# A fused attention, transform and mixer kernel: the last batch's transform begun after the attention's steps, two product blocks ahead of it, and the first normalization spread over the steps

## The chip, the cores and the metric

The kernel runs on one core of a Trainium2 chip, with its five engines: TensorE (PE, matmuls; PEld is its weight load), VectorE (DVE), ScalarE (ACT), GpSimd (POOL) and SyncE (SP, which issues the transfers). Each engine runs its own queue in order, and engines wait for each other by semaphores. The metric is the time of one execution on the device in microseconds, median of three runs; smaller is better.

## The reference

Batch 4, 8 heads, 576 tokens, head size 64, model width 512. Three parts follow each other, the output of one being the input of the next:

```python
# attention in a window of 64 tokens
scores = where(mask, scale * q @ k.T, -1e9)
x = softmax(scores) @ v                      # heads side by side: (4, 576, 512)
# first mixer
mixed = real(fft(fft(x, axis=1), axis=2))
u = x + mixed
un = (u - mean(u)) / sqrt(var(u) + 1e-6)
x = u + relu(un @ w_ch1) @ w_ch2             # 512 -> 2048 -> 512
# second mixer
u = x + (relu(x.T @ w_tok1) @ w_tok2).T      # over the tokens, 576 -> 256 -> 576
out = u + relu(u @ w_ch1) @ w_ch2            # 512 -> 1536 -> 512
```

The weights come as 64-bit floats.

## The kernel before

**Attention, steps.** The work is cut into 36 units (4 batches, 9 units each: a tile of 128 tokens and half the heads). `front_body` runs 39 steps k, software-pipelined: in step k ScalarE does the exponentials of unit k (`a_ex`), TensorE transposes the result of unit k-1 into `pt` (`a_pt`) and multiplies that of unit k-2 by the values into `o` (`a_pv`), VectorE divides (`a_nx`), and TensorE makes the scores `s` of unit k+1, whose row maxima `mx` VectorE takes and ScalarE scales to `nb`. Everything in the front is put into each engine's queue in the order of the code (`manual_schedule`); the rest of the program is ordered by a scheduler.

**Transform.** As soon as a batch's units are done, VectorE folds its rows (`fold`, `fold_m`: tiles pmt, eo, then xh and xs, the latter for the last 64 rows, each split into a high and a low part by a ScalarE cast and a VectorE subtraction, L128 and L131). `fft(b)` is a generator of 16 pieces: the first-stage products `zp` (L531; eight matmuls in two pieces each), `zpx`, and then `bp` and `ap`, after each of which VectorE and GpSimd add the result to x. `chunk()` hands out the next piece; each step takes two.

**Normalization and first product.** `prep` yields part by part: row statistics (L664), an inverse root in small VectorE operations (L638 to L647), then for each of three tiles the normalized rows `una` (ScalarE, L679), their transposition `tpa` (TensorE, L685) and the split into `aT`. A group is 384 tokens. `side0` holds the generator of group 0, `pre1` that of group 1. In the steps, parts are taken while a budget of VectorE time, `left`, lasts. `gphase` then runs, for group g and feature block f, a first product `zg` (L694, 12 matmuls), its relu on ScalarE (L701) and VectorE's low part `hh` (L702), and, three blocks later, the second product into `acc` (L712, 9 matmuls). Called one zg block at a time, it makes 32 such blocks for groups 0 and 1, in the middle with the groups taking turns; two buffers hold zg.

**Weights.** `converter` turns each 64-bit weight tile into 32-bit in three parts, one for each call of `conv`: first ScalarE's L163 and VectorE's L164, L165, L166; then VectorE's L179 and L180 and a multiplication L182 on GpSimd (on VectorE late in the tail, when `tailing` exceeds 10); then, for the tile before, the low part L185 on VectorE, whose high part ScalarE casts (L175). 32 tiles are converted for this product, the first few in the attention's steps, the others while zg blocks run: `gphase` takes two parts between the first product and its hh, and one more behind it outside the tail.

**Tail.** After the steps a loop takes what is left of the last transform piece by piece, with a zg block ahead of every fourth piece, a conversion part after every odd one and a part of `pre1` after every even one from the fourth on. Then zg blocks follow without anything between.

Of the kernel before, what the change touches and what calls it, by code (L numbers as in the profile page):

```python
# [29 lines left out]
def kernel(  # L30
# [19 lines left out]
    B, H, S, D = 4, 8, 576, 64  # L50
# [13 lines left out]
    def blk(shape, dt=F32, name="blk"):  # L64
        return sb.tile(shape, dt, tag="blk", bufs=32 - CFG["nqv"], name=name)
# [22 lines left out]
    def cvm(shape, dt=F32, name="cvm"):  # L88
        return sb.tile(shape, dt, tag="cvm", bufs=2, name=name)
# [36 lines left out]
    def split(hi, lo, src, hi_eng, lo_eng):  # L126
        if hi_eng is nc.scalar:
            nc.scalar.copy(out=hi, in_=src)  # L128
        else:
            hi_eng.tensor_copy(out=hi, in_=src)  # L130
        lo_eng.tensor_tensor(out=lo, in0=src, in1=hi.bitcast(F32), op=ALU.subtract)  # L131
# [62 lines left out]
    tailing = [0]  # L194
# [4 lines left out]
    def conv(n):  # L199
        for _ in range(n):  # L200
            if conv_g[0] is None:
                if not jobs:
                    return
                conv_g[0] = converter()
            conv_s[0] = next(conv_g[0], 1)
            if conv_s[0] == 1:
                conv_g[0] = None
            if conv_s[0] == "wait":
                return
# [284 lines left out]
    def fold_m(b):  # L494
        h0 = 64 * (b % 2)
        a, z = slice(h0, h0 + 64), slice(64 - h0, 128 - h0)
        x = x_t[b, 4]
        eo = cvm([128, 2, 257], F32, name="eo")
        eng = nc.vector
        eng.tensor_tensor(out=eo[a, 0, 1:256], in0=x[a, 1:256], in1=x[a, 511:256:-1], op=ALU.add)  # L500
        eng.tensor_tensor(out=eo[a, 1, 1:256], in0=x[a, 1:256], in1=x[a, 511:256:-1], op=ALU.subtract)
        for e in range(2):
            nc.vector.tensor_scalar(
                out=eo[a, e, 0:257:256], in0=x[a, 0:257:256], scalar1=2.0, scalar2=None, op0=ALU.mult
            )
        yield 1.0
        h = blk([128, 2, LN], F32R, name="xs")
        split(h[a, :, 0:257], h[z, :, 0:257], eo[a], nc.scalar, nc.vector)
        fst[b, 2] = h
        yield 0.6  # L510
# [178 lines left out]
    def gemm1(W, f, res):  # L689
        zp = pg("zg")[:, 0:GT]  # L690
        n = 0
        for d in range(4):
            for a, c in PASSES:
                nc.tensor.matmul(zp, lhsT=W[f, 0][:, a, d, :], rhs=res["aT"][:, c, d, :], start=n == 0, stop=n == 11)  # L694
                n += 1
        res["z", f] = zp
# [132 lines left out]
    def drain(gen):  # L829
        for _ in gen:  # L830
            pass
# [101 lines left out]
    if True:  # L933
# [19 lines left out]
        def gphase(l, W, NF, src, dst, norm, extra):  # L953
            if l == 0:
                res[1, 0]["pool"] = pm
                res[0, 0]["first"] = res[1, 0]["first"] = True
                seq = [(g, f) for g in range(2) for f in range(KA)] + [(g, f) for f in range(KA, NF - 3) for g in range(2)]
                seq += [(g, f) for g in range(2) for f in range(NF - 3, NF)]
                g0 = 2
            else:  # L960
                seq = []
                g0 = 0
            seq += [(g, f) for g in range(g0, NG) for f in range(NF)]
            nxt = pre1[0] if l == 0 else prep(l, src, 1, norm, res[1, l])
            for g, f in seq:
                r = res[g, l]
                if g and f == 0:
                    drain(nxt)
                    nxt = iter(())
                while l == 0 and ((f, 0) not in W or (f, 1) not in W):  # L970
                    conv(1)
                gemm1(W, f, r)
                if manual[0]:
                    conv(2)
                gemm1_ev(W, f, r)
                pend.append((l, W, f, NF, r, g, src, dst))
                second(CFG["lag"])
                if g + 1 < NG and f == CFG["pf"] and g >= g0 and g > 0:
                    nxt = prep(l, src, g + 1, norm, res[g + 1, l])
                elif l == 0 and g == 1 and f == CFG["pf2"]:  # L980
                    nxt = prep(l, src, 2, norm, res[2, l], False, pg)
                elif manual[0] and g < 2 and f > CFG["pf2"]:
                    late = g == 1 and f >= NF - 3
                    for _ in range(2 if late else 1):
                        if late or ncount[0] < 8:
                            next(nxt, None)
                            ncount[0] += 1
                else:
                    next(nxt, None)
                extra(g, f)  # L990
                if l == 0 and g == 1 and f == NF - 1:
                    phase2[0] = True
                yield
            second(0)
# [30 lines left out]
        def front_body():  # L1025
# [12 lines left out]
            side = []  # L1038
            ffts = []
            cur = []  # L1040
            evs = []
            side0 = []
            pcount = qcount = 0
            left = 0.0

            def chunk():
                while cur or ffts:
                    if not cur:
                        cur.append(fft(ffts.pop(0)))
                    e = next(cur[0], None)  # L1050
                    if e is not None:
                        return e
                    cur.pop()
                return None

            for k in range(NU + 3):
# [14 lines left out]
                left = min(left, 0.0) + CFG["dve"] - (1.5 if k < NU else 0.7)  # L1071
# [5 lines left out]
                if 0 <= k - 2 < NU:  # L1077
                    b, t, par = units[k - 2]
                    if par == 1 and t in (1, 3):
                        side.append(fold(b, t // 2))  # L1080
                    if t == 4:
                        side.append(fold_m(b))
                while side and left > 0.0:
                    t = next(side[0], None)
                    if t is None:
                        side.pop(0)
                    else:
                        left -= t
# [33 lines left out]
                while side0 and left > 0.0 and (pcount < 7 or k >= 28):  # L1122
                    t = next(side0[0], None)
# [13 lines left out]
            while side0:  # L1137
                if next(side0[0], None) is None:
                    side0.pop(0)
            n = 0  # L1140
            tailing[0] = 1
            while True:
                if n % 4 == 0:
                    next(gph)
                e = chunk()
                if e is None:
                    break
                e()
                if n % 2:
                    conv(1)  # L1150
                elif n >= 4:
                    next(pre1[0], None)
                put_stores()
                n += 1
                tailing[0] = n + 1
# [7 lines left out]
        fdone = set()  # L1163
# [65 lines left out]
        k = CFG["wb0"]  # L1229
# [155 lines left out]
```

## Time and profile before

| | |
|---|---|
| median of 3 runs | 977.66 us (977.2 to 978.43) |
| the profiled execution | 978.04 us, its span 976.3 us |
| TensorE busy | 938.4 us (96% of the span) |
| VectorE busy | 613.9 us (63%) |
| ScalarE busy | 349.6 us (36%) |
| GpSimd busy | 120.6 us (12%) |

The busy shares are averages over stages with different limits: attention with transforms until about 172 us of the span, the tail until about 210 us, zg blocks with weight conversions until about 310 us, and then the products and the second mixer. A matmul's end is modelled, so a busy TensorE need not run at its peak.

### The profile page before, as it was taken

Reading aid. Unit: us, or ns where it says so; the run is one execution under the profiler, and the core shown is the slowest. Engines: PE = TensorE matmul, PEld = TensorE weight load, DVE = VectorE, ACT = ScalarE, POOL = GpSimd, SP = SyncE. Lnnn points to the kernel's source line nnn. Section 1 sums busy time; section 2 is a strip of 40 time slices with the busy share of each in tenths; the row PEclk is TensorE's granted clock in tenths of the full one; section 3 lists DMA queues with packets and bytes.
Section 4 is the critical chain, followed back from the end, with each engine's and each line's share of the span. In section 5 each row is a group of like instructions: output and inputs, shape, how many; then the busy total and the mean of one; then the engine's idle time right before and its main releaser. Section 6 shows DMA issues by size and latency. Waiting matters only on the chain.

```text
span 976.3 us, 16237 instructions
## 1 busy us (share of the span) xinstructions
PE 938.4 (96%) x6413; PEld 831.2 (85%) x6413; DVE 613.9 (63%) x1343; ACT 349.6 (36%) x761; POOL 120.6 (12%) x128
## 2 busy tenths in 40 slices
PE   9898987799999999999999999989999999999997
PEld 5586765788888899989999988867999999999997
DVE  3887778799997365577675324445865445444544
ACT  4664553423333222232131322324443333333332
POOL 0003213142221011112111000011400000000000
PEclk9997999799999999999999999999999999999999
DMA  9853221344442243444534206375311011101000
GB/s 332 319 151 133 67 67 47 89 137 128 140 120 75 71 140 91 158 166 151 191 130 130 87 25 224 117 226 176 105 44 44 1 44 44 44 1 45 23 22 22
DMA packets 58192, 105.61 MB, mean 108 GB/s; under 512 B 5250, under 2 KB 25796, under 8 KB 57732
## 3 DMA queue, kind: packets, MB, share of 16 engines
q1 hardware_dynamic: 57428, 104.25, 33.1%
q8 instruction: 50, 0.82, 0.4%
q10 hardware_dynamic: 688, 0.33, 0.1%
q14 instruction: 26, 0.21, 0.1%
HBM read 79.78 MB, written 24.77 MB: 107 GB/s over the span
## 4 chain that ended last, share of the span: by engine, by line
PE 64%; DVE 14%; DMA 3%; issue 2%; ACT 1%; POOL 0%; DVEq 0%; SPq 0%; ACTq 0%; POOLq 0%
PE zg L694 15%; PE acc L712 15%; PE zg L729 15%; PE acc L773 11%; PE acc L760 3%; DVE wm L180 2%; PE zt L890 2%; DVE we L166 2%; PE tpa L685 1%; PE zt L915 1%; DVE w2s L185 1%; DMA x2r<-x_d 1%; DVE w1s L185 1%; DVE rw L179 1%; DVE hh L702 1%
## 5 line engine op out<-in xcount | busy, mean ns | idle before, releaser
L694 PE MATMUL zg<-aT,w1s 128*128 128x384 f32 x1152 | 224.8, 343 | 3.8 <-DVE hh L702 2.8
L694 PEld LDWEIGHTS zg<-aT,w1s 128*128 128x128 f32 x1152 | 203.8, 190 | 20.3 <-DVE hh L702 12.9
L712 PE MATMUL acc<-w2s,hh 128*128 128x512 f32 x864 | 218.7, 395 | 0.0
L712 PEld LDWEIGHTS acc<-w2s,hh 128*128 128x128 f32 x864 | 160.9, 188 | 29.7
L729 PE MATMUL zg<-aT,wb 128*128 128x256 f32 x1296 | 165.2, 282 | 1.0 <-ACT wb L128 1.0
L729 PEld LDWEIGHTS zg<-aT,wb 128*128 128x128 f32 x1296 | 158.2, 188 | 2.0 <-ACT wb L128 1.2
L182 POOL TENSOR_TENSOR wm<-wm,we 128x512 f32<-128x512 f32 (+2 forms) x64 | 70.5, 1101 | 343.4 <-DVE wm L180 247.4
L702 DVE SCALAR_TENSOR_TENSOR hh<-zg,hh 128x384 fp32r<-128x384 f32 x96 | 53.3, 555 | 88.1 <-ACT hh L701 88.0
L701 ACT ACTIVATE hh<-zg 128x384 fp32r<-128x384 f32 x96 | 46.9, 489 | 168.9 <-PE zg L694 168.6
L773 PE MATMUL acc<-wb,hb 128*128 128x256 f32 x540 | 71.4, 280 | 0.0
L163 ACT ACTIVATE wm<-rw 128x512 f32<-128x512 uint32 (+2 forms) x66 | 41.7, 632 | 81.9 <-DVE w2s L185 38.9
L773 PEld LDWEIGHTS acc<-wb,hb 128*128 128x128 f32 x540 | 67.1, 188 | 0.0
L736 ACT ACTIVATE h<-zg 128x512 f32<-128x512 f32 x54 | 32.3, 598 | 96.8 <-PE zg L729 90.7
L747 DVE TENSOR_TENSOR s4h<-h 128x128 f32<-128x128 f32 x90 | 23.2, 299 | 58.8 <-ACT h L736 58.6
L773 PE MATMUL acc<-wb,ha 128*128 128x256 f32 x405 | 56.7, 282 | 0.0
L773 PEld LDWEIGHTS acc<-wb,ha 128*128 128x128 f32 x405 | 51.9, 189 | 0.2
L131 DVE TENSOR_TENSOR hb<-s4h,hb 128x512 fp32r<-128x512 f32 x45 | 31.2, 693 | 28.2 <-ACT hb L128 28.2
L180 DVE SCALAR_TENSOR_TENSOR wm<-rw,wm 128x512 f32<-128x512 int32 (+2 forms) x66 | 43.4, 658 | 5.5 <-ACT wm L163 0.4
L166 DVE SCALAR_TENSOR_TENSOR we<-rw,we 128x512 uint16<-128x512 uint16 (+2 forms) x66 | 43.5, 660 | 2.0
L128 ACT CAST hb<-s4h 128x512 fp32r<-128x512 f32 x45 | 27.9, 621 | 39.8 <-PE acc L773 32.3
L414 PE MATMUL s<-kT,qT 64*64 64x128 f32 x576 | 41.4, 285 | 0.0
L433 ACT ACTIVATE pb<-s,nb 128x128 f32<-128x128 f32 x144 | 40.9, 369 | 0.2
(151 smaller groups left out, 1202.9 us busy)
## 6 DMA issues: line engine op xcount, KB each, us to landing
rw<-in_moe_w_ch_dram SPq DMA_DIRECT2D x56, 512.0 KB, 3.6
vt<-in_vx_dram SPq DMA_DIRECT2D x16, 520.0 KB, 5.8
ur<-u_d SPq DMA_DIRECT2D x28, 256.0 KB, 3.6
wb_d<-wm SPq DMA_DIRECT2D x24, 256.0 KB, 2.9
rf<-wb_d SPq DMA_DIRECT2D x24, 256.0 KB, 3.3
kT<-in_kt_dram SPq DMA_DIRECT2D x3, 1536.0 KB, 10.6
qT<-in_qt_dram SPq DMA_DIRECT2D x8, 512.0 KB, 5.0
x_d<-o SPq DMA_DIRECT2D x16, 256.0 KB, 4.2
```

Source lines behind the costliest of these rows:

```text
L163: held("a", nc.scalar.activation(out=m, in_=low, func=AF.Copy, scale=2.0 ** -52, bias=1.0))
L166: nc.vector.scalar_tensor_tensor(out=e, in0=top, scalar=0x8000, in1=e, op0=ALU.bitwise_and, op1=ALU.bitwise_or)
L180: nc.vector.scalar_tensor_tensor(out=m, in0=high, scalar=2.0 ** -20, in1=m, op0=ALU.mult, op1=ALU.add)
L182: eng.tensor_tensor(out=m, in0=m, in1=e.bitcast(BF16), op=ALU.mult)
L414: nc.tensor.matmul(s4[64 * bl:64 * bl + 64, c, :], lhsT=q_t[b, t // 2][64 * r:64 * r + 64, c, q0:q0 + 64], rhs=kT[b][64 * r:64 * r + 64, c ...
L433: nc.scalar.activation(out=pb[:, 0, c], in_=s4[:, c], func=AF.Exp, bias=nb[:, c:c + 1], scale=scale)
L694: nc.tensor.matmul(zp, lhsT=W[f, 0][:, a, d, :], rhs=res["aT"][:, c, d, :], start=n == 0, stop=n == 11)
L701: nc.scalar.activation(out=h[:, 0], in_=zp, func=AF.Relu)
L702: nc.vector.scalar_tensor_tensor(out=h[:, 1], in0=zp, scalar=0.0, in1=h[:, 0].bitcast(F32), op0=ALU.max, op1=ALU.subtract)
L712: nc.tensor.matmul(res["acc"][c], lhsT=h[:, a, 128 * c:128 * c + 128], rhs=W[f, 1][:, w, :], start=f == 0 and i == 0, stop=f == NF - 1 and ...
L729: nc.tensor.matmul(zp[:, j], lhsT=WB[2 * p + j, 0][:, a, d, :], rhs=res["aT"][:, c, d, :], start=n == 0, stop=n == 11)
L773: nc.tensor.matmul(res["acc"][k][:, 256 * half:256 * half + 256], lhsT=t[:, a, e, :], rhs=c[i][w], start=p == 1 and n == 0 and i in (0, 4) ...
```

## The change

```diff
@@ gphase
-                else:
+                elif not tailing[0]:
                     next(nxt, None)
@@ chunk
                 while cur or ffts:
                     if not cur:
+                        if ffts[0] == B - 1 and not tailing[0]:
+                            return None
                         cur.append(fft(ffts.pop(0)))
@@ the steps, ahead of the folds
+                if k >= 28 and side0:
+                    t = next(side0[0], None)
+                    if t is None:
+                        side0.pop(0)
+                    else:
+                        left -= t
                 while side and left > 0.0:
@@ after the steps
             while side0:
                 if next(side0[0], None) is None:
                     side0.pop(0)
+            for t in side:
+                drain(t)
+            if B - 1 not in fdone:
+                fdone.add(B - 1)
+                ffts.append(B - 1)
             n = 0
             tailing[0] = 1
             while True:
-                if n % 4 == 0:
+                if n in (0, 1, 5, 9, 13):
                     next(gph)
                 e = chunk()
@@
                 if n % 2:
                     conv(1)
-                elif n >= 4:
+                else:
                     next(pre1[0], None)
```

From step 28 on one part of group 0's normalization is taken in each step whatever the budget says, ahead of the folds; the old budgeted loop stays and may take another in the same step. The last batch's transform hands out no piece before the tail, where all 16 stand now (14 before); the tail puts zg blocks ahead of pieces 0, 1, 5, 9 and 13 in place of 0, 4, 8 and 12, and takes a part of `pre1` after every even piece, while `gphase` takes none there.

What this makes of the queues is shown at three places. ScalarE, attention steps 29 to 31 (s_1801 is the scores' tile of unit 30, the exponentials of which are pb; zt is the split of zp). Before:

```order
L425 ACTIVATE nb<-mx 128x4
L128 CAST xs<-eo 64x2x257
L679 ACTIVATE una<-x,nm,y 128x512
L433 ACTIVATE pb<-s_1801,nb 128x128 x4
L443 COPY pb<-pt 128x512
L425 ACTIVATE nb<-mx 128x4
L128 CAST zt<-zp 128x320
L128 CAST aT<-tpa 128x4x128
L433 ACTIVATE pb<-s_1849,nb 128x128 x4
```

Now:

```order
L425 ACTIVATE nb<-mx 128x4
L128 CAST aT<-tpa 128x4x128
L128 CAST xs<-eo 64x2x257
L433 ACTIVATE pb<-s_1801,nb 128x128 x4
L443 COPY pb<-pt 128x512
L425 ACTIVATE nb<-mx 128x4
L128 CAST zt<-zp 128x320
L679 ACTIVATE una<-x,nm,y 128x512
L128 CAST aT<-tpa 128x4x128
L433 ACTIVATE pb<-s_1855,nb 128x128 x4
```

The first una has gone into step 28, and in step 30 (and again in step 31) una and the cast aT of its transposition stand next to each other, behind zt and ahead of the next exponentials.

TensorE, the start of the tail, behind the last matmul of batch 2's transform. Before:

```order
L577 MATMUL ap<-nyq,zx 64x258 x2
L531 MATMUL zp<-cs_hi,xh 128x320
L531 MATMUL zp<-cs_lo,xh 128x320
L531 MATMUL zp<-cs_hi,xh 128x320 x2
L531 MATMUL zp<-cs_lo,xh 128x320
L531 MATMUL zp<-cs_hi,xh 128x320
L531 MATMUL zp<-cs_hi,xs 128x320
L531 MATMUL zp<-cs_lo,xs 128x320
L685 MATMUL tpa<-ident,una 128x128 x4
L694 MATMUL zg<-aT,w1s 128x384 x12
```

Now:

```order
L577 MATMUL ap<-nyq,zx 64x258 x2
L694 MATMUL zg<-aT,w1s 128x384 x12
L531 MATMUL zp<-cs_hi,xh 128x320
L531 MATMUL zp<-cs_lo,xh 128x320
L531 MATMUL zp<-cs_hi,xh 128x320 x2
L694 MATMUL zg<-aT,w1s 128x384 x12
L531 MATMUL zp<-cs_lo,xh 128x320
L531 MATMUL zp<-cs_hi,xh 128x320
L531 MATMUL zp<-cs_hi,xs 128x320
L531 MATMUL zp<-cs_lo,xs 128x320
```

Two zg blocks have moved ahead of the matmuls that read xs, and the last tpa of group 0 has left this place.

VectorE, the repeating pattern behind the tail, from the sixth zg block on. Before:

```order
L185 TENSOR_TENSOR w2s<-wm,w2s 128x512
L164 TENSOR_SCALAR we<-rw 128x512
L165 TENSOR_SCALAR we<-we 128x512
L166 SCALAR_TENSOR_TENSOR we<-rw,we 128x512
L179 TENSOR_SCALAR rw<-rw 128x512
L180 SCALAR_TENSOR_TENSOR wm<-rw,wm 128x512
L702 SCALAR_TENSOR_TENSOR hh<-zg,hh 128x384
```

Now:

```order
L185 TENSOR_TENSOR w2s<-wm,w2s 128x512
L164 TENSOR_SCALAR we<-rw 128x512
L165 TENSOR_SCALAR we<-we 128x512
L166 SCALAR_TENSOR_TENSOR we<-rw,we 128x512
L702 SCALAR_TENSOR_TENSOR hh<-zg,hh 128x384
L179 TENSOR_SCALAR rw<-rw 128x512
L180 SCALAR_TENSOR_TENSOR wm<-rw,wm 128x512
```

hh has moved from between L180 and L185 to between L166 and L179. Counted from the start, the 25th hh had 31 sets of L164 to L166 and 29 times L185 ahead of it; it now has 32 and 30. The statistics and root operations of group 2 stand directly behind hh in both.

## Rows read from the trace of the kernel before

**Rows 1.** Stretches: length; busy us of PE, PEld, DVE, ACT, POOL; PEclk; DMA.

```profile
172.00:210.00 38.00, 33.91 (x174) 30.29 (x174) 32.11 (x61) 15.94 (x31) 12.81 (x13) 0.85 0.34 108
219.00:305.00 86.00, 84.05 (x399) 70.38 (x399) 81.69 (x151) 30.54 (x58) 21.63 (x19) 1.00 0.42 126
```

**Rows 2.** Timeline, one step: start us, length us, engine, line, operation, [idle before, releaser].

```profile
240.00 0.69 DVE L180 SCALAR_TENSOR_TENSOR wm<-rw,wm 128x512 f32<-128x512 int32 x1
240.61 0.55 DVE L702 SCALAR_TENSOR_TENSOR hh<-zg,hh 128x384 fp32r<-128x384 f32 x1
240.77 1.16 POOL L182 TENSOR_TENSOR wm<-wm,we 128x512 f32<-128x512 f32 x1 [3.28 <-DVE wm L180]
241.07 1.41 DVE L185 TENSOR_TENSOR w2s<-wm,w2s 128x512 fp32r<-128x512 f32 x1
241.21 2.06 PEld L694 LDWEIGHTS zg<-aT,w1s 128*128 128x128 f32 x12 [0.40 <-DVE hh L702]
...
242.41 0.41 DVE L164 TENSOR_SCALAR we<-rw 128x512 uint16<-128x512 uint16 x1
...
243.91 0.43 DVE L179 TENSOR_SCALAR rw<-rw 128x512 int32<-128x512 int32 x1
244.44 0.69 DVE L180 SCALAR_TENSOR_TENSOR wm<-rw,wm 128x512 f32<-128x512 int32 x1
```

**Rows 3.** Timeline of TensorE, two zg blocks after the last conversion.

```profile
314.16 2.27 PE L694 MATMUL zg<-aT,w1s 128*128 128x384 f32 x12
...
318.35 2.28 PE L694 MATMUL zg<-aT,w1s 128*128 128x384 f32 x12
```

**Rows 4.** Timeline of VectorE, the 6th and the 25th hh.

```profile
218.40 0.55 DVE L702 SCALAR_TENSOR_TENSOR hh<-zg,hh 128x384 fp32r<-128x384 f32 x1
...
304.85 0.55 DVE L702 SCALAR_TENSOR_TENSOR hh<-zg,hh 128x384 fp32r<-128x384 f32 x1
```

**Rows 5.** Timelines of TensorE and ScalarE, attention steps.

```profile
141.45 0.82 ACT L679 ACTIVATE una<-x,nm,y 128x512 f32<-128x512 f32 x1
...
143.42 0.42 PE L531 MATMUL zp<-cs_hi,xh 128*128 128x320 f32 x1
...
145.15 0.41 ACT L128 CAST zt<-zp 128x320 fp32r<-128x320 f32 x1
...
147.19 0.42 PE L531 MATMUL zp<-cs_hi,xh 128*128 128x320 f32 x1
...
151.83 0.60 PE L685 MATMUL tpa<-ident,una 128*128 128x128 f32 x4
```

**Rows 6.** VectorE's waits, 171.7 to 210 us: in total, times, longest.

```profile
DVE zt L131 <- ACT zt L128: 2.8, 3, 1.4
DVE aT L131 <- ACT aT L128: 1.1, 2, 0.6
DVE hh L702 <- ACT hh L701: 0.8, 1, 0.8
```

**Rows 7.** Timelines of VectorE and GpSimd in the tail.

```profile
183.79 0.69 DVE L180 SCALAR_TENSOR_TENSOR wm<-rw,wm 128x512 f32<-128x512 int32 x1
184.40 0.69 DVE L185 TENSOR_TENSOR w1s<-wm,w1s 128x512 fp32r<-128x512 f32 x1
184.62 1.49 POOL L182 TENSOR_TENSOR wm<-wm,we 128x512 f32<-128x512 f32 x1 [5.08 <-DVE wm L180]
185.00 1.39 DVE L164 TENSOR_SCALAR we<-rw 128x512 uint16<-128x512 uint16 x1
...
187.36 0.55 DVE L702 SCALAR_TENSOR_TENSOR hh<-zg,hh 128x384 fp32r<-128x384 f32 x1
```

**Rows 8.** Timeline of VectorE, a step with row statistics of group 2.

```profile
276.67 0.68 DVE L664 BATCH_NORM_STATS2 st<-ur 128x6 f32<-128x512 f32 x1
...
277.49 0.66 DVE L185 TENSOR_TENSOR w2s<-wm,w2s 128x512 fp32r<-128x512 f32 x1
...
281.19 0.69 DVE L664 BATCH_NORM_STATS2 st<-ur 128x6 f32<-128x512 f32 x1
```

## The prediction

> **What bounds the kernel now.** The stretches of the profile come first. From 219 to 305 us VectorE is busy for 81.69 of 86.00 us and TensorE, with ends that are modelled, for 84.05; from 172 to 210 us TensorE's granted clock averages 0.85, so part of it ran at the lower of its two levels, 1.2 GHz [rows 1]. The reader is to see that both engines look full late, and that something is open early. The timeline of one step settles which of the two leads: VectorE's instructions follow one another without a gap, L180 to L180 takes 4.44 us, and the weight loads of the next zg begin 0.05 us after VectorE's hh of L702 has ended [rows 2]. TensorE then needs 4.19 us a step once no conversion is left [rows 3]. So from the end of the attention to about 305 us VectorE's queue sets the pace, zg block after zg block, and hh of L702 is the handle by which it holds TensorE. The 6th hh starts at 218.40 us and the 25th at 304.85 us: 86.45 us for 19 steps [rows 4]. One more hh behind that, TensorE runs on its own. Whatever the change does is therefore read in one number: by how much later or earlier the 25th hh comes.
>
> **The change part by part.** The order shows no instruction added or taken away on any engine, and TensorE's order is the same from the sixth zg on. All is motion, so every term is waiting, or a position in VectorE's queue. I take four terms.
>
> 1. *The parts of the first normalization, one or two per attention step from step 28.* One step of the attention is one run of pt, o, s and zp on TensorE, 143.42 to 147.19, 3.77 us [rows 5]. Before, una stands in one step and its transposition tpa in a later one, so neither waits. Now ScalarE has una and the cast aT in one step, behind the cast zt, which waits for the step's last zp; and TensorE has tpa ahead of the next pt. That closes a ring: end of zp, cast zt 0.41, una 0.82, tpa 0.60, and only then the next pt [rows 5]. TensorE stands still for the first two and spends the third there: 1.83 us a step, in steps 30 and 31, 3.7 us. Queued behind the waiting cast aT on ScalarE is the next softmax, but it is wanted only a step later, so it adds nothing. The first part, in steps 28 and 29, delays the max of step 30 by nothing, because VectorE has the fold to do meanwhile; the fold's xs comes later by one set of divisions and a maximum, and against that step 34 is rid of its tpa. These two I set against each other. Bounds: nothing, if the slack of the rotation (a softmax is used a step later) covers the ring, and 7 us, if TensorE falls to 1.2 GHz in the gaps and the 3.77 us of each of the two steps nearly double. I take +3.7.
>
> 2. *The last transform begun after the steps, two zg blocks in its place.* Between 171.7 and 210 us VectorE waits 2.8 us for ScalarE's cast of zt, 1.1 us for that of aT and 0.8 us for the relu ahead of hh, 4.7 us together [rows 6]. They stem from TensorE, which begins the transform's first zp only when xs is there. Now two zg blocks run while VectorE still folds, the folds and then a conversion stand ahead of the first hh, and two more conversion parts go in between. Walking VectorE's new order with these durations I find it fed nearly throughout; what is left is about 0.7 us around the third and fourth zp, whose accumulators wait for VectorE itself. Bounds: all 4.7 us recovered, or none, if each wait returns at the next cast. I take -4.0.
>
> 3. *The place of hh in VectorE's queue.* With five zg blocks in the tail in place of four, and each taking two conversion parts along, the repeating pattern comes out turned: hh now stands between L166 and L179, where it stood between L180 and L185. Before the 25th hh (and every one from the 7th) VectorE has now done one more set L164 to L166 and one more L185. The set is 242.41 to 243.91, 1.50 us [rows 2], an unhindered L185 0.60 us [rows 7]. As VectorE is the bound, that is +2.1 us. It would be nothing if TensorE were the bound; that is a rival below.
>
> 4. *What follows GpSimd's multiplication.* After L180 GpSimd starts L182. In the old order the first thing VectorE does meanwhile is hh, which is not slowed; then L185 takes from 241.07 to 242.41, 1.34 us, since it ends only behind GpSimd's [rows 2]. With statistics in between, L185 takes 0.66 us [rows 8]: the cover costs no time, it uses the held time. In the new order L180 is followed at once by L185 and L164, with hh gone. That succession occurs once in the tail of before: L185 is quick, GpSimd's multiplication stretches to 1.49 us, and L164 starts at 185.00 and ends 0.28 us behind GpSimd's end at 186.11, after 1.39 us [rows 7] in place of about 0.42. From L180 to the place of hh that is 183.79 to 187.36, 3.57 us [rows 7]; with hh's own 0.46 (240.61 to 241.07) and L179's 0.53 (243.91 to 244.44) a step is 4.56 us, against 4.44 [rows 2]. Of the 19 steps between 6th and 25th hh 16 cost 0.12 more, 1.9 us. The three that carry statistics take 4.52 us now, because L664 fills held time; in the new order they stand where nothing is held and add their full 0.82 us, 276.67 to 277.49 [rows 8]: 4.56 + 0.82 - 4.52 = 0.86 each, 2.6 us. Together +4.5. Bounds: the lower is that L164 is not held at all, which is the second rival; the upper is +7, if a plain step costs not 0.12 but 0.24 us more, because L166 holds its follower as long as in the old order (0.73 in place of 0.61).
>
> A rule speaks against this edit. The Trainium skill, SBUF — State Buffer, section "Who interferes with whom", says that VectorE and GpSimd share one port pair as an exclusive lock, that the first to come keeps it for its whole instruction while the other blocks fully, and that a VectorE instruction with at most one input in SBUF, outside the two-port modes, stays out of it. Rows 7 and 2 agree in kind. Taken literally it has GpSimd's 1.16 us begin only when L185 ends, 1.30 us behind L180, so L164 would be free at 2.46 in place of the row's 2.32: 0.14 us more a step, 2.7 us over 19, and the sum below would be 9.0 and the time 986.7 us, still inside the forecast's own case.
>
> Sum: 3.7 - 4.0 + 2.1 + 4.5 = +6.3 us. The profiled execution took 978.04 us, so 984.3; the median of the three runs is 0.4 below it, and the forecast is stated against that: 977.66 + 6.3 = **984.0 us**.
>
> **The rivals.** *The attention's slack covers term 1.* For it: each softmax is consumed a step later, and VectorE waits in those steps already. Against it: the ring runs through TensorE's in-order queue, where tpa stands ahead of pt. Then the sum is 2.6, 980.3 us.
> *L164 is not held, and VectorE stops being the bound.* The place is the pair L185, L164 behind L180 in the 19 steps. For it: a lone instance in the tail is all that shows the hold. Without its 0.98 us a step of VectorE is 3.6 us, less than TensorE's 4.19 [rows 3]; TensorE then sets 19 x 4.19 = 79.6 us in place of 86.45, -6.8 for term 4, and the sum is 3.7 - 4.0 + 2.1 - 6.8 = -5.0, 972.7 us: faster. It decides the sign where the hold is 6.3/19 = 0.33 us shorter than that instance, at 0.65 us. Against it: the instance is clean, and 1.39 us is more than three times 0.42.
> *TensorE's clock falls more often.* For it: the average of 0.85 [rows 1] with waits of a few us, and the ring of term 1 opens gaps of 1.2 us and more. Two steps at half speed cost up to 3.8 us each; half of that is +3.5 or so on top, 987.5 us. Against it: where VectorE bounds, a slow zg is hidden.
>
> **How the numbers follow.** About 0.2%, 2 us, is what a measurement of this kernel can tell from no change. The forecast's case (980.5 to 987) gets 0.58; the covered attention 0.16, of which 0.10 slower and 0.06 inside 2 us; L164 not held 0.16, 0.11 faster and 0.05 the same in its partial forms; the slower clock 0.10. So slower 0.58 + 0.10 + 0.10 = 0.78, same 0.11, faster 0.11. The range takes in the covered attention down to 978.3 and the clock up to 988.5, and leaves the unheld L164 and a tenth of the worst out.
>
> **What would show it.** Term 1: two attention steps near 136 to 149 us of some 5.6 us, with TensorE idle ahead of tpa for una. Term 2: VectorE's waits between xs and the fifth hh near 1 us. Terms 3 and 4: L185 near 0.69 us and L164 near 1.4 us all along from the 6th hh, steps of about 4.56, statistics steps of about 5.4, and the 25th hh at some 311 us with zg behind it at once. The prediction is wrong if L164 stays near 0.42, if the steps fall to 4.2, or if xs ends no later than before.

## The result, and the profile after

The changed kernel took 983.46 us, median of 6 runs (981.98 to 987.53), against 978.11 us for 6 runs of the kernel before: a ratio of 1.0062, with a 95% interval of 1.0048 to 1.0076. It is slower, and the forecast was 984.0 us. The profiled execution took 981.98 us with a span of 980.2 us, the fastest of the six, which matters below.

The stretches that answer to [rows 1], with the same columns, in the changed kernel:

```profile
172.00:210.00 38.00, 27.05 (x130) 24.39 (x130) 35.86 (x67) 17.25 (x33) 13.22 (x12) 0.78 0.36 108
219.00:305.00 86.00, 81.49 (x387) 68.10 (x386) 83.35 (x146) 30.54 (x55) 26.01 (x18) 1.00 0.40 121
```

VectorE is fuller in both (35.86 against 32.11, 83.35 against 81.69), TensorE emptier, and the granted clock of the first is lower, 0.78 against 0.85; but the tail begins later now, so the first stretch is not the same work in the two kernels. The 6th and the 25th hh, answering to [rows 4], on VectorE's timeline of the changed kernel:

```profile
221.76 0.56 DVE L702 SCALAR_TENSOR_TENSOR hh<-zg,hh 128x384 fp32r<-128x384 f32 x1 [0.42 <-ACT hh L701]
...
311.54 0.55 DVE L702 SCALAR_TENSOR_TENSOR hh<-zg,hh 128x384 fp32r<-128x384 f32 x1
```

The 25th comes 6.69 us later than before, and the 19 steps take 89.78 us, 3.33 more. But the starts of a span vary. The last common event is the row maximum of unit 29 in step 28 (125.60 us here, 126.62 before); against that the 25th hh is 7.71 us late. The table below gives, for each trace, this maximum's start and how long behind it xs (the last fold's low part), the 6th and the 25th hh start, all from VectorE's timelines; it is the yardstick for all that follows. The maxima of steps 28, 30 and 32 and xs, before:

```profile
126.62 0.69 DVE L423 TENSOR_REDUCE mx<-s 128x4 f32<-128x512 f32 x1
...
135.53 0.68 DVE L423 TENSOR_REDUCE mx<-s 128x4 f32<-128x512 f32 x1
...
144.33 0.68 DVE L423 TENSOR_REDUCE mx<-s 128x4 f32<-128x512 f32 x1
...
170.97 0.69 DVE L131 TENSOR_TENSOR xs<-eo,xs 64x514 fp32r<-64x514 f32 x1 [0.68 <-ACT xs L128]
```

and in the changed kernel:

```profile
125.60 0.69 DVE L423 TENSOR_REDUCE mx<-s 128x4 f32<-128x512 f32 x1
...
136.26 0.68 DVE L423 TENSOR_REDUCE mx<-s 128x4 f32<-128x512 f32 x1
...
149.04 0.69 DVE L423 TENSOR_REDUCE mx<-s 128x4 f32<-128x512 f32 x1 [0.35 <-PE s L414]
...
175.68 0.69 DVE L131 TENSOR_TENSOR xs<-eo,xs 64x514 fp32r<-64x514 f32 x1 [0.68 <-ACT xs L128]
```

The table (a number in front is that of an experiment below):

| trace | maximum | xs | 6th hh | 25th hh | 19 steps |
|---|---|---|---|---|---|
| before | 126.62 | 44.35 | 91.78 | 178.23 | 86.45 |
| changed | 125.60 | 50.08 | 96.16 | 185.94 | 89.78 |
| changed, second trace | 126.60 | 53.42 | 99.50 | 189.27 | 89.77 |
| 1: parts per step alone | 126.20 | 48.36 | 96.06 | 182.53 | 86.47 |
| 2: tail alone | 126.35 | 44.23 | 90.47 | 180.25 | 89.78 |
| 3: changed, two parts fewer | 126.12 | 48.36 | 91.67 | 180.66 | 88.99 |
| 3, second trace | 126.33 | 48.36 | 91.68 | 179.96 | 88.28 |
| 4: before, two parts more | 126.09 | 44.20 | 94.56 | 184.29 | 89.73 |
| 5: changed, una and tpa apart | 126.23 | 43.80 | 89.93 | 179.69 | 89.76 |
| 6: changed, short L182 | 125.64 | 50.08 | 91.99 | 170.55 | 78.56 |
| 7: tail alone, two fewer | 125.66 | 44.06 | 87.94 | 176.19 | 88.25 |
| 9: apart, two fewer | 126.02 | 45.07 | 88.35 | 176.72 | 88.37 |
| 10: tail alone, five fewer | 126.08 | 44.29 | 86.64 | 171.39 | 84.75 |
| 12: changed, two other parts left out | 126.54 | 53.42 | 99.97 | 189.73 | 89.76 |

Three places make the 7.71 us. **The attention**, on the timelines of TensorE and ScalarE in step 30 of the changed kernel, answering to [rows 5]:

```profile
137.37 0.43 ACT L128 CAST zt<-zp 128x320 fp32r<-128x320 f32 x1 [0.19 <-PE zp L531]
137.69 0.81 ACT L679 ACTIVATE una<-x,nm,y 128x512 f32<-128x512 f32 x1
138.56 1.11 PE L685 MATMUL tpa<-ident,una 128*128 128x128 f32 x4 [1.23 <-ACT una L679]
139.47 1.06 PE L440 MATMUL pt<-ident,pb 128*128 128x128 f32 x4
...
145.94 0.66 PE L685 MATMUL tpa<-ident,una 128*128 128x128 f32 x4 [1.23 <-ACT una L679]
```

This is the ring of the prediction: zt, una, tpa, and only then pt, with TensorE idle for 1.23 us in each of two steps. The first tpa takes 1.11 us where the same four matmuls took 0.60 in [rows 5], the second 0.66: in the first of the two steps the clock is at the lower of its two levels, in the second at the higher one. xs comes 5.73 us later than before. Of this 1.75 us stand ahead of the ring: the maximum of step 30 is 10.66 us behind that of step 28, before 8.91. The next two steps, which hold the ring, take 12.78 us in place of 8.80, 3.98 more.

**The tail.** From xs to the 6th hh it is 46.08 us against 47.43, although 2.1 us of conversions have been put ahead. The timelines split this: VectorE waits 5.00 us there before (the 4.7 of [rows 6] and 0.3 for TensorE's ap) and 0.42 now, 4.58 less; the rest of its time is 45.66 us in place of 42.43, 3.23 more, the 2.1 and another 1.1 by which its instructions take longer. VectorE's waits between xs and the 6th hh, answering to [rows 6], and TensorE's from 128 to 215 us (in total, times, longest):

```profile
DVE xs L131 <- ACT xs L128: 0.7, 1, 0.7
```

```profile
PE zg L694 <- DVE w1s L185: 5.5, 1, 5.5
PE tpa L685 <- ACT una L679: 4.9, 3, 2.5
PE zpx L544 <- DVE zt L131: 4.5, 1, 4.5
```

VectorE waits for nothing once xs is there until 0.42 us ahead of the 6th hh; instead TensorE waits for VectorE, 5.5 us in the second zg block alone, whose weight is now converted only behind the folds. VectorE is busy all that time, so this wait is not what sets the tail's length.

**The steps.** One step behind the tail in the changed kernel, answering to [rows 2]:

```profile
240.70 0.69 DVE L180 SCALAR_TENSOR_TENSOR wm<-rw,wm 128x512 f32<-128x512 int32 x1
241.31 0.69 DVE L185 TENSOR_TENSOR w2s<-wm,w2s 128x512 fp32r<-128x512 f32 x1
...
241.54 1.49 POOL L182 TENSOR_TENSOR wm<-wm,we 128x512 f32<-128x512 f32 x1 [3.01 <-DVE wm L180]
241.91 1.40 DVE L164 TENSOR_SCALAR we<-rw 128x512 uint16<-128x512 uint16 x1
...
244.28 0.55 DVE L702 SCALAR_TENSOR_TENSOR hh<-zg,hh 128x384 fp32r<-128x384 f32 x1
244.75 0.42 DVE L179 TENSOR_SCALAR rw<-rw 128x512 int32<-128x512 int32 x1
244.88 0.30 PEld L694 LDWEIGHTS zg<-aT,w1s 128*128 128x128 f32 x2 [0.49 <-DVE hh L702]
```

L164, not L185, now ends 0.28 us behind GpSimd's multiplication, and the step takes 4.50 us. A step with statistics, answering to [rows 8]:

```profile
275.77 0.55 DVE L702 SCALAR_TENSOR_TENSOR hh<-zg,hh 128x384 fp32r<-128x384 f32 x1
276.24 0.68 DVE L664 BATCH_NORM_STATS2 st<-ur 128x6 f32<-128x512 f32 x1
...
278.70 1.40 DVE L164 TENSOR_SCALAR we<-rw 128x512 uint16<-128x512 uint16 x1
...
281.07 0.55 DVE L702 SCALAR_TENSOR_TENSOR hh<-zg,hh 128x384 fp32r<-128x384 f32 x1
```

The statistics stand outside the held time and L164 is long all the same: 5.30 us in place of 4.52.

In this one execution 3.8 of the 7.7 us are missing from the span, most of them in two places: the maximum of unit 29 came 1.02 us earlier, and the stretch between two transpositions of the second mixer, 641.01 to 674.94 us, took 33.93 us in place of 36.44. No instruction has moved there: 1.38 us are a run of 17 matmuls of L890 (4.36 us against 5.74), nearly all the rest two waits for x2h (2.63 against 3.82). In the second trace of the same kernel that stretch took 35.95, and over all traces 32.8 to 37.3, with no order by edit (36.9 and 37.3 for the two traces of the third experiment's kernel); it is spread between executions. It is sorted by the granted clock: 1.00 in the four traces of up to 35.0 us (changed, 2, 5 and 9), 0.95 in the ten from 35.6 us on.

### The profile page after: what moved, and what is told of

The parts are those of the page before. It is cut to its first block, busy times and chain, and to the rows that moved or that the text cites. A ratio compares the mean times of both kernels' runs of the same rounds, so it can differ in the third digit from the quotient of the medians.

```text
span 980.2 us, 16240 instructions
## 1 busy us (share of the span) xinstructions
PE 937.9 (96%) x6413; PEld 831.3 (85%) x6413; DVE 618.4 (63%) x1343; ACT 352.5 (36%) x761; POOL 126.4 (13%) x128
## 4 chain that ended last, share of the span: by engine, by line
PE 66%; DVE 25%; ACT 3%; DMA 3%; issue 2%; POOL 0%; SPq 0%; DVEq 0%; ACTq 0%; POOLq 0%
PE acc L712 15%; PE zg L694 15%; PE zg L729 15%; PE acc L773 11%; DVE we L164 3%; PE acc L760 3%; DVE wm L180 2%; DVE we L166 2%; DVE mx L423 2%; PE zt L890 2%; PE tpa L685 1%; DVE rw L179 1%; DVE hh L702 1%; PE zt L915 1%; PE s L414 1%
## 5 line engine op out<-in xcount | busy, mean ns | idle before, releaser
L182 POOL TENSOR_TENSOR wm<-wm,we 128x512 f32<-128x512 f32 (+2 forms) x64 | 77.4, 1209 | 341.1 <-DVE wm L180 231.9
L164 DVE TENSOR_SCALAR we<-rw 128x512 uint16<-128x512 uint16 (+2 forms) x66 | 48.3, 732 | 0.6 <-POOL wm L182 0.4
L180 DVE SCALAR_TENSOR_TENSOR wm<-rw,wm 128x512 f32<-128x512 int32 (+2 forms) x66 | 43.5, 659 | 3.9
L166 DVE SCALAR_TENSOR_TENSOR we<-rw,we 128x512 uint16<-128x512 uint16 (+2 forms) x66 | 43.8, 663 | 2.0
```

The costliest lines, as they stand in the source:

```text
L164: held("c", nc.vector.tensor_scalar(out=e, in0=top, scalar1=0x7FF0, scalar2=None, op0=ALU.bitwise_and))
L166: nc.vector.scalar_tensor_tensor(out=e, in0=top, scalar=0x8000, in1=e, op0=ALU.bitwise_and, op1=ALU.bitwise_or)
L180: nc.vector.scalar_tensor_tensor(out=m, in0=high, scalar=2.0 ** -20, in1=m, op0=ALU.mult, op1=ALU.add)
L182: eng.tensor_tensor(out=m, in0=m, in1=e.bitcast(BF16), op=ALU.mult)
```

## The experiments

The times of before were taken along with each set of runs: 977.42 us (17 runs) for 1 to 4, 977.91 (22) for 5 to 8, 977.90 (17) for 9 to 12. Runs 11 and 12 are one execution each.

**1. The parts per step alone**, on the kernel before.

```diff
+                if k >= 28 and side0:
+                    t = next(side0[0], None)
...
                 while side and left > 0.0:
```

> The kernel before with nothing but the normalization's part per step from step 28. The ring theory (una and its transposition in one attention step, TensorE idle behind both): xs about 5.7 us later against the unit maxima of step 29, as in the changed kernel, the tail and the steps of 4.44 us behind it as before; 3.7 to 5.7 us on top of the kernel before, 981.8 to 983.8 us. Rival, slack: the softmax rotation absorbs it elsewhere, within 1 us of before, 977 to 979 us, and the later xs of the changed kernel stems from the transform's removal from the steps.

983.65 us, ratio 1.0071 (1.0054 to 1.0087): +6.2. xs is 4.01 us later than before, the 25th hh 4.30, steps 4.44. The slack rival falls: the edit alone makes the kernel as slow as the whole change. Of the 4.01 us 1.75 are there by the maximum of step 30, as in the changed kernel, and 2.27 come in the next two steps (11.07 us in place of 8.80). The median is 1.9 us above what the trace explains; the eleventh run bears on that.

**2. The tail alone**: the changed kernel without that insertion.

> The changed kernel without the normalization's part per step. If the terms add up: waits of the tail recovered -3.5, two sets more ahead of the hh's +2.1, dearer steps +3.3, sum +1.9 us over the kernel before, about 980.0 us, with xs where before had it. Rival, all loss is in the tail and the attention's lateness is recovered later: +5.3 us, 983.4 us. Rival, two zg blocks in front are worth more than the turned pattern costs: under 977 us.

978.99 us (11 runs), ratio 1.0017 (1.0006 to 1.0028): +1.6, and the 25th hh +2.02. The terms add up as the first theory said; xs is where before had it.

**3. The changed kernel with two conversion parts fewer at the end of the tail.**

```diff
-                if n % 2:
+                if n % 2 and n < 12:
                     conv(1)
```

> The changed kernel with the last two conversion parts of the tail left to the zg blocks behind it, so that the old pattern comes back (L180, hh, L185, L164) and no hh has more conversions ahead of it than before. Theory (place of hh 2.1, GpSimd's hold on L164 3.3): steps 4.44 us in place of 4.50, statistics steps 4.52 in place of 5.30, L164 0.42, L185 1.41, and 5.4 us less than the changed kernel, about 978.1 us. Rival, only the order of the pattern counts: 3.3 us less, 980.2 us. Rival, the hold returns on L185 and the parts come back behind: no change, 983.5 us.

983.6 us, ratio 1.0064 (1.0049 to 1.0079): no gain, where 5.4 us were expected. The trace has the old pattern, steps of 4.44 us, and the 25th hh 5.28 us earlier than the changed kernel's; but its own execution took 981.22 us, and the five others 982.6 to 986.2. Two things are seen. The two parts had covered a transfer: VectorE now waits 2.5 us for the raw tile ahead of the 7th hh. And 1.72 us of the 5.28 are the attention (48.36 against 50.08), where nothing was edited. In this code an odd piece without a conversion part takes a part of `pre1` instead; in 3, 7 and 9 that leaves TensorE's order as it was. What the medians hide needed more runs: 5 and 7 to 9, 11.

**4. The kernel before with two conversion parts more.**

```diff
                 if n % 2:
-                    conv(1)
+                    conv(3 if n == 13 else 1)
```

> The kernel before with two more conversion parts behind the tail's last odd piece, which turns the pattern as in the changed kernel with no other edit. Theory: L164 1.4 us, L185 0.69, steps 4.50, statistics steps 5.30, +2.1 +3.3 = 5.4 us over the kernel before, about 983.5 us. Rival, the dearer step is a consequence of the tail's or the attention's new order: steps stay 4.44 and only the 2.1 us of the two parts show, 980.2 us.

983.64 us, ratio 1.0062 (1.0047 to 1.0077): +6.2, and the 25th hh +6.06. The turned pattern came with its 4.50 us steps (19 steps 89.73 us, +3.28), in the tail and attention of the kernel before. The parts themselves cost 2.8 us up to the 6th hh in place of 2.1: one of the two multiplications that moved ahead now falls where the kernel puts it on VectorE (late in the tail), 0.7 us. The rival falls.

**5. una and its transposition in different steps**: in the changed kernel the budgeted loop takes no part from step 28.

```diff
-                while side0 and left > 0.0 and (pcount < 7 or k >= 28):
+                while side0 and left > 0.0 and pcount < 7 and k < 28:
```

> The changed kernel with exactly one part of the normalization per attention step from step 28 (the budgeted loop takes none there), so that una and its transposition stand in different steps. Ring theory: TensorE no longer waits for una in steps 30 and 31, the maxima of units 31 to 34 come 3 to 4.3 us earlier against that of unit 29, and the time is as much below the changed kernel's, about 979.5 us; pattern, steps of 4.50 and 5.30 us as in the changed kernel. Rival, the part per step itself delays the maxima through ScalarE and VectorE, in whatever step it stands: no change, 983.5 us.

978.52 us (12 runs), ratio 1.0015 (1.0003 to 1.0026): 4.9 us under the changed kernel, and xs at 43.80 us, as early as before. TensorE's transpositions in this trace:

```profile
129.81 1.09 PE L685 MATMUL tpa<-ident,una 128*128 128x128 f32 x4 [2.47 <-ACT una L679]
140.35 0.60 PE L685 MATMUL tpa<-ident,una 128*128 128x128 f32 x4
148.33 0.60 PE L685 MATMUL tpa<-ident,una 128*128 128x128 f32 x4
```

The first part's wait of 2.47 us holds up the maximum of step 30 by 1.77 us, as in the changed kernel, but the next two steps take 7.10 us in place of 8.80 and make it good; the two waits of 1.23 us were the ring, and they are gone. Against these 7.10 us the ring costs 3.97 in run 1. A part per step cost nothing at xs where una and tpa stood apart.

**6. GpSimd's multiplication over 32 columns in place of all**, in the changed kernel; the exponents of the other columns are left out.

```diff
-                eng.tensor_tensor(out=m, in0=m, in1=e.bitcast(BF16), op=ALU.mult)
+                eng.tensor_tensor(out=m[:, 0:32], in0=m[:, 0:32], in1=e.bitcast(BF16)[:, 0:32], op=ALU.mult)
```

> The changed kernel with GpSimd's multiplication L182 over 32 columns of each weight tile in place of all; the exponents of the other columns are left out. If L164 is long because GpSimd holds it: L164 0.42 us all along, VectorE's step 3.5 us, so that TensorE's 4.19 us sets the pace; 19 steps 80 to 82 us in place of 89.8, and 8 to 9 us less than the changed kernel, about 975 us. Rival, L164 is long for its own operands or for the transfers that write the raw tiles: it stays at 1.4 us and the time at 983.5 us.

971.84 us, ratio 0.9947 (0.9929 to 0.9965): 11.6 under the changed kernel. VectorE's step in this trace:

```profile
242.02 0.69 DVE L180 SCALAR_TENSOR_TENSOR wm<-rw,wm 128x512 f32<-128x512 int32 x1
242.63 0.69 DVE L185 TENSOR_TENSOR w2s<-wm,w2s 128x512 fp32r<-128x512 f32 x1
243.23 0.47 DVE L164 TENSOR_SCALAR we<-rw 128x512 uint16<-128x512 uint16 x1
...
245.00 0.56 DVE L702 SCALAR_TENSOR_TENSOR hh<-zg,hh 128x384 fp32r<-128x384 f32 x1 [0.25 <-ACT hh L701]
```

and TensorE's:

```profile
240.48 2.28 PE L694 MATMUL zg<-aT,w1s 128*128 128x384 f32 x12
...
244.69 2.28 PE L694 MATMUL zg<-aT,w1s 128*128 128x384 f32 x12
```

L164 is 0.47 us with the same operands, the same transfers and the same neighbours on VectorE: the 0.93 us were the multiplication's. hh waits for its relu, and TensorE's zg blocks follow each other at 4.21 us without a wait while VectorE makes a step in 3.91: VectorE is no longer the bound, and the 25th hh, 15.39 us earlier, no longer measures the time. The gain exceeded the 8 to 9 us expected; the tail's conversions are held too (the 6th hh is 4.17 us earlier).

**7. The tail alone, with the two parts fewer**: the edits of 2 and 3 together.

> The changed kernel without the normalization's part per step, and with the last two conversion parts of the tail left to the zg blocks behind it: what is left of the change is the later start of the last transform with its two zg blocks in front. Theory: only the tail's recovered waits remain, 25th hh 3.4 us earlier than in the kernel before against the same maximum, 974.0 us. Rival, what the two parts fewer gain up to the 25th hh is lost again behind it (the fourth experiment's mirror image, the third, showed no gain in its median): 979 us.

975.12 us (10 runs), ratio 0.9978 (0.9966 to 0.9989): faster than before by 2.8 us, and 3.9 below the second experiment. xs to the 6th hh, with as many conversions ahead as before, is 43.88 us in place of 47.43, 3.55 less: VectorE's waits there are 1.41 us in place of 5.00, and the rest of its time is the same to 0.1 us, although one multiplication has gone back from VectorE to GpSimd (0.7 us on VectorE). Of the 5.4 us 1.7 are paid back in one wait, on VectorE's timeline of this kernel:

```profile
214.07 1.36 DVE L185 TENSOR_TENSOR w1s<-wm,w1s 128x512 fp32r<-128x512 f32 x1
217.14 0.43 DVE L164 TENSOR_SCALAR we<-rw 128x512 uint16<-128x512 uint16 x1 [1.71 <-DMA rw<-in_moe_w_ch_dram]
```

**8. The third kernel again.**

> The third experiment's kernel once more, for a second trace. Its trace had the 25th hh 5.4 us earlier than the changed kernel's, against the same maximum, but the median was no lower. If this was a matter of single executions (granted clock in the attention and behind 640 us), the second set has a median of 979 to 981 us and a trace with the same steps of 4.44 us; if the gain is lost again by the kernel itself, the median is 983 to 984 us again, and this trace shows where: a later 25th hh against the maximum of unit 29, or more than 37 us between the transpositions near 636 and 673 us.

The traced execution took 980.09 us at a granted clock of 0.979, the three others 984.76 to 985.36 at 0.970; median 984.8, ratio 1.0067 (1.0046 to 1.0088). The trace repeats the first one to 0.7 us at the 25th hh. Neither of the two places that I had named shows a loss: what costs 5 us is in the executions that were not traced, and goes with their clock.

**9. Both remedies**: the edits of 3 and 5 in the changed kernel.

> The third experiment's kernel with one part of the normalization per attention step, so that both remedies stand together. If the third's gain behind the attention was real and was lost to executions at a lower granted clock that the ring of una and its transposition brings along: 4.0 us less than the fifth experiment, as between the second and the seventh, 974.5 us, with granted clocks of 0.975 and above. Rival, the two parts fewer gain nothing where the part per step stands in the attention: 978.5 us.

976.29 us (12 runs), ratio 0.9982 (0.9968 to 0.9995), 7.3 us below the third kernel, and 2.2 below the fifth, not 4.0; the trace has 2.97 us between the two. The direction is the theory's, the size short. Its xs is 1.27 us later than the fifth's in the traces, from the attention, where the two have the same order; its granted clock from 130 to 150 us is 0.83, the fifth's 0.92.

**10. Five parts fewer**, in the kernel of 2: four odd pieces of the tail without a part, and one part in place of two in one block.

```diff
-                    conv(2)
+                    conv(1 if not tailing[0] and (g, f) == (0, 5) else 2)
...
-                if n % 2:
+                if n % 2 and n < 8:
```

> The seventh experiment's kernel with three conversion parts fewer still ahead of the hh's: four odd pieces of the tail without a part, and one part where two stood in the block of group 0, feature block 5 and above, so that from the 11th hh on one whole tile less stands ahead of each, in the old order. If every part ahead costs VectorE's time up to the last conversion: one set 1.5, L179 and L180 1.1, L185 0.6 us less, less the 0.25 us by which the one more block is slower than TensorE's own, about 3 us under the seventh, 972.2 us; the blocks between 6 and 11 are in the dearer order and give some 0.3 back. Rival, the raw tiles' transfers set the pace then (the seventh waited 1.7 us for one): 975 us or more.

970.23 us, ratio 0.9921 (0.9905 to 0.9936): 7.7 us faster than before and 4.9 under the seventh, where 3 were expected. No wait for a raw tile is left. (Here the parts of `pre1` in place of conversions also bring one tpa forward; this was not separated.) The blocks from the 6th to the 10th, which I had counted as dear, are the cheapest of all; their order is L180, L185, hh, L164, here on the timelines of VectorE and GpSimd:

```profile
219.86 0.69 DVE L180 SCALAR_TENSOR_TENSOR wm<-rw,wm 128x512 f32<-128x512 int32 x1
220.47 0.68 DVE L185 TENSOR_TENSOR w2s<-wm,w2s 128x512 fp32r<-128x512 f32 x1
...
220.63 1.56 POOL L182 TENSOR_TENSOR wm<-wm,we 128x512 f32<-128x512 f32 x1 [2.67 <-DVE wm L180]
221.07 0.55 DVE L702 SCALAR_TENSOR_TENSOR hh<-zg,hh 128x384 fp32r<-128x384 f32 x1
221.54 0.93 DVE L164 TENSOR_SCALAR we<-rw 128x512 uint16<-128x512 uint16 x1
...
224.09 0.69 DVE L180 SCALAR_TENSOR_TENSOR wm<-rw,wm 128x512 f32<-128x512 int32 x1
```

L180 to L180 is 4.23 us, without a wait: two instructions pass quickly ahead of the held one, and only 0.5 us of hold is left. It is the fastest version of the study.

**11. The changed kernel's second trace.**

> The changed kernel once more, for a second trace. If the attention's price of 5.7 us was 4.0 us of ring and 1.7 us of granted clock: xs 48.4 or 50.1 us behind the maximum of unit 29, with a clock between 130 and 150 us of 0.83 or 0.69, and statistics steps and plain steps of 5.30 and 4.50 us as before; the stretch between the transpositions near 641 and 675 us, 33.9 us in the first trace, nearer the 36 us of the other kernels.

988.23 us, xs 53.42 us behind the maximum, neither of the two values expected. The steps are the first trace's (19 in 89.77 us). The stretch from 130 to 150 us, columns as in [rows 1], in this trace:

```profile
130.00:150.00 20.00, 17.12 (x104) 13.33 (x105) 9.45 (x24) 9.99 (x28) 0.00 (x0) 0.55 0.10 27
```

and in the changed kernel's first, and in the eighth run:

```profile
130.00:150.00 20.00, 17.54 (x144) 13.70 (x143) 11.17 (x29) 11.18 (x32) 0.00 (x0) 0.69 0.11 27
```

```profile
130.00:150.00 20.00, 17.30 (x159) 13.47 (x161) 11.55 (x30) 12.47 (x36) 0.00 (x0) 0.83 0.10 27
```

One order of instructions, three granted clocks, 0.83, 0.69 and 0.55, and xs at 48.36, 50.08 and 53.42 us. TensorE's transpositions in the second trace show where:

```profile
139.56 1.12 PE L685 MATMUL tpa<-ident,una 128*128 128x128 f32 x4 [1.23 <-ACT una L679]
...
148.70 1.12 PE L685 MATMUL tpa<-ident,una 128*128 128x128 f32 x4 [1.23 <-ACT una L679]
```

and in the eighth run:

```profile
139.30 0.66 PE L685 MATMUL tpa<-ident,una 128*128 128x128 f32 x4 [1.23 <-ACT una L679]
...
144.95 0.66 PE L685 MATMUL tpa<-ident,una 128*128 128x128 f32 x4 [1.23 <-ACT una L679]
```

In the second trace both stand at the lower level, in the first one of them (1.11 and 0.66 us), in the eighth run none. From the one to the other it takes 9.14, 7.38 and 5.65 us.

**12. Meant as the third kernel's third trace.**

> The third experiment's kernel, a third trace. Two traces had the 25th hh at 180.0 and 180.7 us behind the maximum of unit 29 and times of 980 and 981 us, while most executions without a trace took 984 to 986 us at a granted clock of 0.965 to 0.970. If this execution is one of those: it shows the stretch whose granted clock is lower than in the other two traces. Otherwise: 980 to 982 us again, and the place stays open.

The kernel that ran was another one: it left out the parts behind pieces 1 and 3 of the tail, not behind the last two, parts of `pre1` take their places, and the zg blocks that need the weight take the conversions at once. Its pattern behind the tail is the changed kernel's (19 steps 89.76 us). So it says nothing of the third kernel's slow executions, which were never traced; it is one more trace of the changed attention: 988.33 us, xs again 53.42 us behind the maximum, clock 0.54 from 130 to 150 us.

## Why the prediction was right

The forecast of 984.0 us and its sign held, and VectorE's queue was the bound as argued. The terms, against the traces:

1. *The attention, +3.7.* That una and tpa in one step make the loss is shown by 1 (alone it makes it) and 5 (una and tpa apart, it is gone), and the rival by which the rotation's slack covers the ring falls with 1. The size is this term's error, and in two ways. The first part, which the prediction let cost nothing, holds up the maximum of step 30 by 1.75 us; and the two ring steps cost 2.27 us against before where the clock is back at the higher level by the first of them (run 1, 4.0 in all), 3.98 in the first trace of the changed kernel (5.7), 7.32 in the second (9.1). The ring steps of 5.75 and 5.30 us in run 8, at the higher level, lie near the 5.6 predicted, but before the same two steps took 4.24 and 4.56 us, not the 3.77 of one run on TensorE (nor is it so that neither una nor tpa waited there: TensorE waits 0.48 us for una ahead of the tpa at 135.16 us); run 5 has 3.20 and 3.90. The prediction also kept the slower clock as a rival of its own, with 0.10, and bounded this term by 7 us. It is no rival but part of the term, in some executions of one and the same kernel: without the ring, six traces (before, 2, 4, 5, 7, 10) have xs at 43.8 to 44.4 us and one (9) at 45.1.

2. *Waits recovered, -4.0.* VectorE's waits between xs and the 6th hh fell from 5.00 to 0.42 us in the changed kernel, -4.58, to 0.96 in run 2 and to 1.41 in run 7. The mechanism holds, and the size nearly.

3. *The place of hh, +2.1.* The rest of VectorE's time up to the 6th hh grew by 3.23 us: the conversions counted as 2.1, and 1.1 more (L164, for one, takes about 1.4 us twice there, once before). With the second term that makes -1.35, and 5.73 - 4.58 + 3.23 + 3.33 = 7.71. Run 4 has 2.8 with one more multiplication on VectorE in it, and taking the parts away again (7) brings a wait of 1.7 us for a raw tile. That the parts ahead buy cover for the transfers was missing from the prediction.

4. *GpSimd's hold, +4.5.* Shown by 6, by 4 and by the steps; the size is 3.3. Plain steps are 0.06 us dearer, not 0.12 (L179 to L180 is 0.45 us behind hh, where I took the 0.53 of the old place), and statistics steps 0.78, not 0.86. The single instance of [rows 7] was a good guide: 1.39 us there, 1.40 here. The rival of an unheld L164 falls; run 6 shows what it would have meant, VectorE's own step at 3.66 us and TensorE's at 4.21, near the 3.6 and 4.19 it was priced with. The literal reading of the rule in the Trainium skill (SBUF — State Buffer, section "Who interferes with whom") gave a step of 4.70 us, 4.62 with L179 as measured. The trace's 4.50 lies under it: L182 ends 1.03 us behind the end of L185, where a multiplication of 1.16 us [rows 2] begun only then would end 0.13 us later. Its record begins 0.23 us behind the start of L185; when it got the port, no row tells. That a VectorE instruction is held until GpSimd is done does agree, with L164 at 1.40 us against 0.47 in run 6.

So the mechanisms held, but the sum came out by errors that cancel, and that is luck: in the first trace the attention cost 5.7 in place of 3.7 and the conversions ahead 3.2 in place of 2.1, GpSimd's hold 3.3 in place of 4.5, and the waits gave back 4.6 in place of 4.0. What can be added up by medians is run 1 (+6.2) and run 2 (+1.6): 7.8 us, against 5.4 to 6.1 for the whole change (medians, ratio); the intervals of the two overlap with that.

What stays open: the third kernel's untraced executions. They lie 4.7 to 5.3 us above the traced one in run 8, and the step from an attention of 48.36 us to one of 53.42 is 5.06 us; with 9, where the ring is away and the median is 7.3 us lower, that is an argument for the attention's clock, not a measurement of it. The clocks on record point the same way: 9 of the 30 executions of kernels with the ring have a mean granted clock of 0.970 or less, and one of more than 110 without it. But the two traces with an attention of 53.42 us have 0.972, so a slow attention alone does not account for the lowest, 0.965. Nor is it known what decides between the three outcomes, or why the clock in the stretch from about 636 to 673 us, which varies by 4.5 us, is 1.00 in some executions and 0.95 in others.

## What to carry to other kernels

Before a part of side work goes into a pipelined step, look whether its producer and its consumer land in the same step on engines that work in order: una and tpa together cost 4 us and more, apart nothing at xs. Where GpSimd multiplies next to a full VectorE, try two instructions that pass quickly between the one that releases GpSimd and the one that is held: L180, L185, hh, L164 made a step of 4.23 us, where one quick one ahead of the held made 4.44 (hh, L185) and 4.50 (L185, L164). Conversions pulled ahead of a bound engine's critical instruction cost their full time there, and cover transfers; take them out step by step and measure. A transfer that shows is no reason to stop: it cost 1.7 us in run 7, and run 10 with three parts fewer still had no such wait and gained another 4.9 us.

## What was not expected of the hardware

The same instructions in the same order ran the stretch from the maximum of unit 29 to xs in one of three durations, 48.36 us (1, 3 and 8), 50.08 (the changed kernel and 6) and 53.42 (11 and 12), with granted clocks from 130 to 150 us of 0.83, 0.69 and 0.54 to 0.55. (Only run 1 differs, in TensorE's last few instructions of that stretch.) All seven have the wait of 1.23 us ahead of each of the two transpositions; the clock falls to its lower level before the first of them in all, and is back ahead of it, between the two, or behind both. The kernel before, with other waits there, has 0.91 and 44.35 us.

GpSimd's multiplication of one size took 1.16 us behind L180 when hh came first on VectorE, 1.49 when L185 and L164 followed, and 1.56 when L185 and hh did. In the two turned orders L164 ended 0.28 us behind it.
